# Another opening for the attention part of a two-stage kernel: where the first four outputs' upper score blocks come from, how the first z is fetched, and when w2 is loaded

## The chip, the cores and the metric

The kernel runs on one core of one Trainium2 chip. A core has a matrix engine (TensorE, PE in the profile; its weight loads are PEld), a vector engine (VectorE, DVE), a scalar engine (ScalarE, ACT), GpSimd (POOL) and a queue engine (SyncE, SP). Here POOL and SP do little but issue transfers. POOL's are made by software and can convert float32 to bfloat16 on the way; SP's are made by hardware and can transpose, but not convert. The metric is the device time of one execution in microseconds, as a median of several runs. The order of the instructions on each engine is the order of the program text: nothing is reordered by a planner, and each engine takes its instructions in that order and waits on semaphores.

## The reference

Eight batches b of 3136 rows. First an attention without softmax, in which z stands on both sides, then a mixer:

```python
scores = (1.0 / S) * np.matmul(z, z.transpose(0, 2, 1))   # (8, 3136, 3136), z has 64 columns
attn = np.maximum(scores, 0.0) ** 2
x = u * np.matmul(attn, v)                                # u, v: (8, 3136, 256)

h = x.transpose(0, 2, 1) @ U @ V                          # rank 32
y = x + h.transpose(0, 2, 1)
out = y + np.maximum(y @ w_ch1, 0.0) @ w_ch2              # 256 -> 1024 -> 256
```

The scores are symmetric: block (j, o) is the transpose of block (o, j). The kernel uses this.

## The kernel before

**Tiles and blocks.** The 3136 rows of a batch are 24 tiles of 128 rows and one tail of 64 (NT = 25, NF = 24, tile t = 24 is the tail). For each tile j a panel `A[j]` holds 13 blocks of 128 columns (NB = 13): the squared, rectified scores of tile j with tiles j, j+1, ..., j+12, counted modulo 25. The other twelve blocks that an output needs are transposes of blocks in its own panel. They come as a `strip` of 12 blocks: `turn(b, o)` (L311) has SP transpose `A[o]` by DMA into one of five strip buffers. `block(b, o, j)` (L345) picks the panel or the strip.

**Scores.** `score` (L272) makes a piece: two matmuls, one on each half of TensorE's rows, that run at the same time (that is why z is kept twice, in partitions 0 to 63 and 64 to 127), into one of two PSUM buffers (`ps2`, two banks each); then ACT rectifies and scales out of PSUM (L291) and VectorE squares in place (L293). A whole panel is two pieces of 832 columns (`score_steps`, L295). Products (`half`, L349, and `beside`, L601) take a block as weights and 256 columns of v as the moving side, again in two row halves. The two halves of TensorE add into two PSUM banks, and two outputs share a pair of banks; `sets` (L97) holds two such pairs. `close_pair` (L360) adds the two banks and multiplies by u: one ACT copy, two VectorE operations.

**z.** The matmuls need z transposed, in `zT` (25 tiles, and the first 12 again behind them, `extend_z` L217). `load_z` (L169) fetches z by POOL with conversion, `double_z` (L182) copies it twice on VectorE, and `turn_z` (L192) transposes by SP. For batch 0 `turn_on_pe` (L199) transposes by matmuls against the unit matrix `eye`, and ACT or VectorE copies the result out of PSUM. For batch 0 zT lies in `zT_first`, in room of `relu_bf` that is idle at that time; other batches use `zT_rest`.

**Order.** Outputs run in the order 12, 13, ..., 24, 0, ..., 11 (`turns`, L132). In each of the 25 steps i of a batch (L783) the products of one output are issued, with pieces of later panels spread between them. `turn(b, turns(i + 4))` is issued at the end of step i. From batch 1 on, the mixer of the batch before is done in bursts at steps 4, 8, 13 and 17; its second matmul, the first reader of w2, is at L562.

**The opening** (`start_up`, L607) is batch 0's first eight outputs, in two groups of four, before that loop begins at step 8 (output 20).
- Group 1, outputs 12 to 15: thirteen `pairs` (L642) of tiles j. For each, the scores of the two tiles j with the four outputs are made (512 columns each), and used two pairs later by four outputs at once. For j = 3 to 11 they are part of a panel and are put there. For the other sixteen (0, 1, 2 and 12 to 24) they are put into `rooms` (L639), in the v buffer of batch 1 and in `x_bf`, and are used only here; the panels of these tiles are made later all the same. Beside them five of the eight pieces of panels 16 to 19 are made (`nxt`).
- Group 2, outputs 16 to 19: the rest of `nxt`, six stored pairs, then a `tail` in which the strips' products, the pieces of panels 20 to 23 (`more`) and the rests of panels 8 to 15 (`rest`, 36 blocks) alternate. w2 is fetched when group 2 opens (L693), and z of batch 1 is doubled and turned whole just after (L695).
- `first_at` (L756) lists what is left for the loop: panels 24, 0, 1, 2, and the first blocks of panels 3 to 11.
- `v_at` (L781) spreads the nine loads of batch 1's v over steps 9 to 23.

Of the kernel before, what the change touches and what calls it, by code (L numbers as in the profile page):

```python
# [42 lines left out]
def kernel(  # L43
# [11 lines left out]
    nc = tc.nc  # L55
# [136 lines left out]
    def turn_z(b, parts):  # L192
        z_bf = z_tiles[b]
        for t0, t1 in parts:
            transpose(
                out=zT_of(b)[:, t0 : upto(t1), :],
                in_=z_bf[:, t0 : upto(t1), :, :].rearrange("p t h c -> p (t h c)"),
            )
    def turn_on_pe(parts, banks):  # L199

        z_bf = z_tiles[0]
        for (t0, t1), ps in zip(parts, banks):
# [8 lines left out]
            copy = nc.vector.tensor_copy if t0 % 8 else nc.scalar.copy  # L211
# [21 lines left out]
    def weight_steps():  # L233
# [21 lines left out]
        def copies():  # L255
# [7 lines left out]
            lambda: wide(w2_bf, moe_w_ch2),  # L263
# [343 lines left out]
    def start_up():  # L607
        parts = ((8, 16), (0, 8), (16, NF))
        load_z(0, parts[:2])
# [10 lines left out]
        load_v(0, (8, 12))  # L620
        load_v(0, (12, 18))
        load_z(0, parts[2:])
        for part in [(3, 8), (0, 3), (18, NF), (NF, NT)]:
            load_v(0, part)
        double_z(0, parts[:2])
        turn_on_pe([(8, 12), (12, 16)], sets[0])
        turn_on_pe([(0, 4), (4, 8)], sets[1])
        nc.gpsimd.memset(U_bf[:, NF, :], 0.0)
        outs = [FIRST + i for i in range(NG)]
        c0 = FIRST * P  # L630
# [5 lines left out]
        for s in fetches[:3]:  # L636
            s()
        nxt = [s for j in range(LEAD, LEAD + NG) for s in turned(0, j)]
        rooms = [v_both[1][:, t : t + 4, :] for t in range(0, NF, 4)]  # L639
        rooms = [r.rearrange("p (a t) d -> p a (t d)", a=2) for r in rooms]  # L640
        rooms += [x_bf[:, g].rearrange("p (a w) -> p a w", a=2) for g in (2, 3)]
        pairs = [(8, 9), (10, 11), (12, 13), (14, 15), (6, 7), (3, 4), (5,), (1, 2)]  # L642
        pairs += [(0, 16), (17, 18), (19, 20), (21, 22), (23, 24)]
        where = {}

        def make(pair):
            if all(LEAD - 1 - HALF <= j < FIRST for j in pair):
                todo = []
                for j in pair:
                    at = (FIRST - j) * P  # L650
                    where[j] = A[j][:, at : at + NG * P]
                    todo.append((j, c0, NG * P, where[j]))
                score(0, todo)
            else:
                room = rooms.pop(0)
                for i, j in enumerate(pair):
                    where[j] = room[:, i, :]
                score(0, [(j, c0, NG * P, room) for j in pair])

        seen = []  # L660

        def use(pair):
            for j in pair:
                for o in outs:
                    at = (o - FIRST) * P
                    stop = [o % 2 == 1 and len(seen) == NT - 1 - h for h in range(2)]
                    beside(o, j, where[j][:, at : at + P], stop)
                seen.append(j)

        for i, pair in enumerate(pairs):  # L670
            if i == 3:
                double_z(0, parts[2:])
            if i == 5:
                ps = pair_psum()
                turn_on_pe([(16, 20), (20, NF)], [ps[:, 0, :], ps[:, 1, :]])
                turn_on_pe([(NF, NT)], [pair_psum()[:, 0, :]])
                extend_z(0)
            make(pair)
            if i > 5 and i % 2:
                nxt.pop(0)()  # L680
            if i > 1:
                use(pairs[i - 2])
        for pair in pairs[-2:]:
            nxt.pop(0)()
            use(pair)
        for o in outs[1::2]:
            close_pair(0, o)
# [187 lines left out]
```

## Time and profile before

| | |
|---|---|
| median of 5 runs | 1015.0 us (1010.15 to 1024.21) |
| the profiled execution | 1013.82 us, its span 1012.1 us |
| PE busy | 991.3 us, 98% of the span |
| ACT busy | 613.8 us, 61% |
| DVE busy | 541.5 us, 54% |
| POOL busy | 172.1 us, 17% |
| chain that ended last | PE 91%, DVE 4%, DMA 2%, ACT 2% |
| products with panel blocks (L351) | 4864 matmuls, 334.6 us busy |
| products with strip blocks (L351) | 4420 matmuls, 306.6 us busy |
| scores (L278, `zT`) | 812 matmuls, 130.7 us busy |

The page gives busy time of each engine as a share of one profiled execution, the chain of waits that ended last, and groups of instructions by line and shape. A matmul's own duration in it (270 ns for a product) is not its price: matmuls overlap, and two row halves run at once, so a row of sixteen is what shows the rate. Durations beside an ACT or VectorE row in the timeline are those of a merged group: "x4" after 2.07 us means four instructions that ended 2.07 us after the first began. "[0.75 <-ACT A L291]" is the idle time of the engine before the row, and what ended it.

### The profile page before, as it was taken

How to read it: one execution, taken by the hardware profiler on the slowest of the kernel's cores; microseconds unless marked ns; L12 is line 12 of the kernel's file. 1: busy time of each engine (PE TensorE's matmuls, PEld its weight loads, DVE VectorE, ACT ScalarE, POOL GpSimd, SP SyncE). 2: the span in 40 equal slices, each digit the busy share in tenths (PEclk: the TensorE clock that was granted, in tenths of full speed). 3: DMA queues.
4: the chain of work that ended last, by engine and by line, in shares of the span. 5: the costliest groups of instructions: out<-in, count | busy, mean ns of one | idle time of the engine just before them, and what ended most of it. 6: DMA issues, size and time to landing. Idle time of an engine off the chain costs nothing.

```text
span 1012.1 us, 31331 instructions
## 1 busy us (share of the span) xinstructions
PE 991.3 (98%) x13856; PEld 783.5 (77%) x13856; DVE 541.5 (54%) x977; ACT 613.8 (61%) x834; POOL 172.1 (17%) x318
## 2 busy tenths in 40 slices
PE   7899999999999999999999999999999999999998
PEld 5678778787778877788787887878877788777856
DVE  5878654456544664446654556445664356542242
ACT  6887764667645776456764667556674666643154
POOL 4122112121121211121112211112112120011000
PEclk9999999999999999999999999999999999999999
DMA  8999989999898998989999998989999998767432
GB/s 156 158 204 222 180 147 194 177 176 155 156 202 170 176 168 171 163 183 171 148 187 165 183 167 146 190 172 189 151 159 194 172 181 142 140 148 166 103 97 97
DMA packets 414584, 167.70 MB, mean 166 GB/s; under 512 B 389408, under 2 KB 399328, under 8 KB 414448
## 3 DMA queue, kind: packets, MB, share of 16 engines
q1 hardware_dynamic: 384944, 99.16, 61.2%
q0 software_dynamic: 29504, 66.55, 28.2%
q8 instruction: 108, 1.77, 0.7%
q14 instruction: 28, 0.23, 0.1%
HBM read 61.88 MB, written 25.69 MB: 87 GB/s over the span
## 4 chain that ended last, share of the span: by engine, by line
PE 91%; DVE 4%; DMA 2%; ACT 2%; issue 1%; DVEq 0%; ACTq 0%; POOLq 0%
PE ps L351 46%; PE ps L562 17%; PE ps L520 17%; PE ps L278 6%; ACT A L291 1%; PE ps L385 1%; DVE A L293 1%; PE ps L442 1%; DVE x_bf L502 1%; DMA ut<-x_bf 1%; PE ps L488 1%; DVE both L366 1%; DMA zT<-z_bf 1%; DVE x_bf L375 0%; DMA strip<-A 0%
## 5 line engine op out<-in xcount | busy, mean ns | idle before, releaser
L291 ACT ACTIVATE A<-ps 128x832 bf16<-128x832 f32 (+8 forms) x469 | 352.8, 763 | 154.5 <-PE ps L278 146.0
L351 PE MATMUL ps<-v,A 64*128 64x256 bf16 x4864 | 334.6, 270 | 4.9 <-DVE A L293 2.8
L293 DVE TENSOR_TENSOR A<-A 128x832 bf16<-128x832 bf16 (+8 forms) x469 | 240.4, 524 | 147.8 <-ACT A L291 144.0
L351 PE MATMUL ps<-v,strip 64*128 64x256 bf16 x4420 | 306.6, 269 | 0.5 <-DMA strip<-A 0.5
L351 PEld LDWEIGHTS <-A 64*128 64x128 bf16 x4864 | 238.7, 94 | 49.5 <-issue 13.6
L538 ACT ACTIVATE relu_bf<-ps 128x1024 bf16<-128x1024 f32 (+2 forms) x208 | 187.9, 909 | 142.9 <-PE ps L520 140.9
L351 PEld LDWEIGHTS <-strip 64*128 64x128 bf16 x4420 | 220.6, 94 | 35.4 <-DMA strip<-A 0.9
L562 PE MATMUL ps<-w_bf,relu_bf 128*128 128x256 bf16 x1600 | 204.7, 273 | 0.2 <-ACT relu_bf L536 0.2
L573 DVE TENSOR_TENSOR o_sb<-ps,x_bf 128x512 f32<-128x512 f32 (+1 forms) x104 | 69.7, 670 | 246.8 <-PE ps L562 237.0
L520 PE MATMUL ps<-ut,w_bf 128*128 128x512 bf16 (+2 forms) x896 | 199.4, 353 | 0.9 <-DMA ut<-x_bf 0.5
L562 PEld LDWEIGHTS <-relu_bf 128*128 128x128 bf16 x1600 | 156.0, 98 | 47.2 <-issue 3.2
L335 POOL DMA_DIRECT2D u_sb<-in_u_dram x96 | 53.8, 560 | 470.0 <-DVE x_bf L375 437.0
L520 PEld LDWEIGHTS <-w_bf 128*128 128x128 bf16 x896 | 85.1, 98 | 61.8 <-issue 6.4
L278 PE MATMUL ps<-zT 64*128 64x416 bf16 (+8 forms) x812 | 130.7, 312 | 0.0
L365 ACT COPY both<-ps 128x512 f32<-128x512 f32 (+1 forms) x104 | 58.8, 566 | 73.2 <-PE ps L351 65.4
L581 POOL DMA_DIRECT2D out_dram<-o_sb x84 | 46.0, 547 | 270.2 <-DVE o_sb L573 266.2
L366 DVE TENSOR_TENSOR both<-ps,both 128x512 f32<-128x512 f32 (+1 forms) x104 | 69.3, 666 | 27.2 <-ACT both L365 26.6
L375 DVE TENSOR_TENSOR x_bf<-both,u_sb 128x512 bf16<-128x512 f32 (+1 forms) x104 | 69.8, 671 | 3.6
L502 DVE TENSOR_TENSOR x_bf<-ps,x_bf 128x512 bf16<-128x512 f32 (+1 forms) x112 | 65.4, 626 | 8.1 <-PE ps L488 8.1
L278 PEld LDWEIGHTS <-zT 64*128 64x128 bf16 x812 | 42.2, 94 | 4.0
L225 POOL DMA_DIRECT2D v<-in_v_dram x61 | 34.0, 559 | 0.2 <-PE ps L520 0.2
L278 PE MATMUL ps<-relu_bf 64*128 64x416 bf16 (+9 forms) x121 | 22.8, 351 | 2.4 <-ACT A L291 1.3
(52 smaller groups left out, 230.7 us busy)
## 6 DMA issues: line engine op xcount, KB each, us to landing
u_sb<-in_u_dram POOLq DMA_DIRECT2D x96, 256.0 KB, 3.8
out_dram<-o_sb POOLq DMA_DIRECT2D x84, 256.0 KB, 3.2
v<-in_v_dram POOLq DMA_DIRECT2D x57, 192.0 KB, 4.4
strip<-A SPq DMA_TRANSPOSE x196, 5.3
out_dram<-o_sb SPq DMA_DIRECT2D x12, 256.0 KB, 2.2
z_c<-in_z_dram POOLq DMA_DIRECT2D x7, 384.0 KB, 5.9
w_bf<-in_moe_w_ch_dram POOLq DMA_DIRECT2D x2, 512.0 KB, 7.5
u_sb<-in_u_dram POOLq DMA_DIRECT2D x16, 64.0 KB, 2.5
```

The costliest lines, as they stand in the source:

```text
L278: mm(out=ps[:, k, :n], lhsT=zT[halves[k], j, :], rhs=zT_flat[halves[k], c : c + n], start=True, stop=True,)
L291: nc.scalar.activation(out=dst, in_=src, func=AF.Relu, scale=sc)
L293: nc.vector.tensor_tensor(out=dst, in0=dst, in1=dst, op=ALU.mult)
L351: mm(out=acc[t0][h][:, (o - t0) * D : (o - t0 + 1) * D], lhsT=w[halves[h]], rhs=v_both[b % 2][halves[h], j, :], start=start, stop=stop, **kw,)
L365: nc.scalar.copy(out=both[:, :w], in_=banks[1][:, :w])
L366: nc.vector.tensor_tensor(out=both[:, :w], in0=banks[0][:, :w], in1=both[:, :w], op=ALU.add)
L375: nc.vector.tensor_tensor(out=x_at(b, t0, n), in0=split(both[:, :w]), in1=u_sb[:, :n, :].rearrange("p t (a c) -> p t a c", c=P), op=ALU.mult,)
L502: nc.vector.tensor_tensor(out=q, in0=split(ps[h][:, : len(ks) * D]), in1=q, op=ALU.add)
L520: mm(out=ps[i][:, :w] if apart else ps[:, i, :w], lhsT=w1_bf[:, db, (hp + i) * P : (hp + i + 1) * P], rhs=uT[c][:, db, len(chunks[c]) * P ...
L538: nc.scalar.activation(out=relus[c][:, hp : hp + 2, :w], in_=ps[:, :, :w], func=AF.Relu)
L562: mm(out=ps[:, k * D : (k + 1) * D], lhsT=relus[c][:, ht, q : q + P], rhs=w2_bf[:, ht, :], start=(ht == 0), stop=(ht == NH - 1),)
L573: nc.vector.tensor_tensor(out=o_sb[:p, :nk, :].rearrange("p t (a c) -> p t a c", c=P), in0=split(ps[:p, : nk * D]), in1=x_at(b, t, nk)[:p] ...
```

## The change

All of it concerns batch 0's opening and what is moved out of its way.

- `first_z` is new. VectorE clears 512 columns of `zT_rest`, and TensorE runs seven matmuls of 512 columns on them, whose result nothing reads. SP fetches z tiles 8 to 15 and 0 to 7 as float32 into the two buffers of u; VectorE converts them into the lower copy of z and ACT into the upper one.
- The third part of z (tiles 16 to 24) is loaded by POOL ahead of all of v. The order of v's parts changes.
- z of batch 1 is loaded as before, then U, V and w1; two parts of v of batch 1 follow at once. w2 is not loaded in the opening, but in two halves at steps 0 and 2 of batch 1.
- Group 1 has 24 steps in place of thirteen pairs. `stored` makes scores of two tiles j below 12 with the four outputs and puts them into the panels. `panel` makes one of the two pieces of a panel, 12 to 17, and turns it by SP from 16 on. `mirror` transposes blocks of `A[o]` on TensorE against `eye` into PSUM, from where VectorE copies them into output o's strip; there are 48 such blocks, in six steps. Nothing is put into `rooms`. The products of a step are issued two steps later. z tiles 16 to 24 are turned ahead of step 2, which makes the first piece of panel 12.
- At step 18 SP reads 8 elements of the second part of batch 1's v into a scratch tile, `mark`.
- Group 2 makes panels 18 to 22, four stored pairs, and the rests of panels 8 to 11 (10 blocks). z of batch 1 is doubled and turned in two parts, after its steps 10 and 12.
- `first_at` then leaves panels 23 and 24 whole and the first blocks of panels 0 to 11. Strips 23, 24 and 0 are turned in steps 8 and 9. Batch 1's other v parts are loaded at every second step from 9 to 21.

```diff
+    def first_z(parts):
+        z_bf = z_tiles[0] = stage.tile([P, NT, 2, dqk], BF16, name="z_bf")
+        wide = zT_rest[:, :4, :].rearrange("p t c -> p (t c)")
+        nc.vector.memset(wide, 0.0)
+        ps = pair_psum()
+        for _ in range(7):
+            mm(out=ps[:, 0, :], lhsT=zT_rest[:, 0, :], rhs=wide, start=True, stop=True)
+        landed = []
+        for t0, t1 in parts:
+            z_f = u_pool.tile([P, 2, D], FP32, name="u_sb").rearrange("p a c -> p (a c)")
+            z_f = z_f.rearrange("p (t c) -> p t c", c=dqk)
+            nc.sync.dma_start(out=z_f, in_=rows(z[0])[:, t0:t1, :])
+            landed.append(z_f)
+        for (t0, t1), z_f in zip(parts, landed):
+            nc.vector.tensor_copy(out=z_bf[:, t0:t1, 0, :], in_=z_f)
+            nc.scalar.copy(out=z_bf[:, t0:t1, 1, :], in_=z_f)
...
-            copy = nc.vector.tensor_copy if t0 % 8 else nc.scalar.copy
+            copy = nc.vector.tensor_copy if t0 % 8 or t1 == NF else nc.scalar.copy
...
-            lambda: wide(w2_bf, moe_w_ch2),
+            lambda: wide(w2_bf[:, NH // 2 :, :], moe_w_ch2[H // 2 :, :]),
+            lambda: wide(w2_bf[:, : NH // 2, :], moe_w_ch2[: H // 2, :]),
...
     def start_up():
-        parts = ((8, 16), (0, 8), (16, NF))
-        load_z(0, parts[:2])
+        first_z(((8, 16), (0, 8)))
         nc.gpsimd.memset(eye, 1.0)
...
-        load_v(0, (8, 12))
-        load_v(0, (12, 18))
-        load_z(0, parts[2:])
-        for part in [(3, 8), (0, 3), (18, NF), (NF, NT)]:
+        load_z(0, ((16, NF),))
+        for part in [(8, 12), (12, 18), (3, 8), (18, NF), (0, 3), (NF, NT)]:
             load_v(0, part)
-        double_z(0, parts[:2])
-        turn_on_pe([(8, 12), (12, 16)], sets[0])
-        turn_on_pe([(0, 4), (4, 8)], sets[1])
...
+        run(fetches[:3])
+        if B > 1:
+            for part in V_PARTS[:2]:
+                load_v(1, part)
+        turn_on_pe([(8, 12), (12, 16)], sets[0])
+        turn_on_pe([(0, 4), (4, 8)], sets[1])
+        extend_z(0)
+        double_z(0, ((16, NF),))
...
+        def mirror(*blocks):
+            def make():
+                flat = pair_psum().rearrange("p a w -> p (a w)")
+                c = 0
+                for o, m0, m1 in blocks:
+                    for m in range(m0, m1):
+                        mm(
+                            out=flat[:, c + (m - m0) * P : c + (m - m0 + 1) * P],
+                            lhsT=A[o][:, (m + 1) * P : (m + 2) * P],
+                            rhs=eye,
+                            start=True,
+                            stop=True,
+                        )
+                    c += (m1 - m0) * P
...
+                    nc.vector.tensor_copy(
+                        out=strips[0, o][:, m0:m1, :].rearrange("p m c -> p (m c)"),
+                        in_=flat[:, c : c + n],
+                    )
...
+        steps = [
+            stored((8, 9), first), stored((10, 11), first),
+            panel(12, 0), panel(12, 1), stored((6, 7), first),
+            panel(13, 0), panel(13, 1), stored((3, 4), first),
+            mirror((12, 0, 8)), panel(14, 0), mirror((13, 0, 8)), panel(14, 1),
+            stored((5, 2), first), stored((1, 0), first), panel(15, 0),
+            mirror((12, 8, 12), (13, 8, 12)), panel(15, 1), mirror((14, 0, 8)),
+            panel(16, 0), mirror((15, 0, 8)), panel(16, 1),
+            mirror((14, 8, 12), (15, 8, 12)), panel(17, 0), panel(17, 1),
+        ]
+        ends = ends_of([e for _, uses in steps for e in uses])
+        for n, (make, uses) in enumerate(steps):
+            if n == 2:
+                turn_on_pe([(16, 20), (20, NF), (NF, NT)], [*sets[0], sets[1][0]])
+            if n == 18 and B > 1:
+                nc.sync.dma_start(out=mark, in_=v_both[1][:1, V_PARTS[1][1] - 1, :8])
+            make()
+            if n > 1:
+                av(steps[n - 2][1], ends)
...
+        todo = [stored(js, LEAD) for js in ((11, 10), (9, 8), (7, 6), (5, 4))]
+        rest = [s for j in range(8, FIRST) for s in score_steps(0, j, LEAD + NG - j, NB)]
+        steps = [
+            (panel(18, 0)[0], []),
+            (panel(18, 1)[0], [(o, j) for j in sides for o in low]),
+            (panel(19, 0)[0], [(o, j) for j in sides for o in high]),
+            (panel(19, 1)[0], own[16] + own[17]),
+            (todo[0][0], []),
+            (todo[1][0], own[18] + own[19]),
...
+        ]
+        for k, s in enumerate(rest):
+            steps.append((s, mirrored[16][3 * k : 3 * k + 3]))
+        for k in range(4):
+            steps.append((panel(21 + k // 2, k % 2)[0], mirrored[17][3 * k : 3 * k + 3]))
+        for o in high:
+            steps.append((None, mirrored[o]))
...
+            if B > 1 and n in (10, 12):
+                part = ((0, FIRST), (FIRST, NF))[n // 2 - 5]
+                double_z(1, (part,))
+                turn_z(1, (part,))
...
-    first_at = {8: [(NT - 1, 0, NB), (0, 0, NB)], 9: [(1, 0, NB)], 10: [(2, 0, NB)]}
-    first_at.update({11: [], 12: []})
-    for j, i in zip(range(3, FIRST), (9, 10, 11, 11, 11, 12, 12, 12, 12)):
+    first_at = {8: [(NT - 2, 0, NB)], 9: [(NT - 1, 0, NB)], 10: [], 11: [], 12: []}
+    for j, i in enumerate((8, 10, 10, 11, 11, 11, 12, 12, 12, 12, 12, 12)):
         first_at[i].append((j, 0, FIRST - j))
+    first_turns = {8: (NT - 2,), 9: (NT - 1, 0)}
...
-        v_at = dict(zip((9, 11, 12, 14, 16, 18, 20, 22, 23), V_PARTS)) if b == 0 else {}
+        v_at = dict(zip((9, 11, 13, 15, 17, 19, 21), V_PARTS[2:]))
...
-            if i + AHEAD < NT:
+            if b == 0 and i in first_turns:
+                for t in first_turns[i]:
+                    turn(b, t)
+            elif i + AHEAD < NT:
                 turn(b, turns(i + AHEAD))
...
+            if b == 1 and i in (0, 2):
+                fetches.pop()()
```

## The prediction

> **What bounds the kernel now.** I read the engine shares first, then busy time in 4 us windows, the timeline of the first 60 us, and the chain that ended last. The page says that TensorE is the bound of the whole: PE 991.3 us of 1012.1, and 91% of the chain. The windows say that the opening is the exception:
>
> ```profile
> core 0: us, PE busy (x) PEld busy (x) DVE busy (x) ACT busy (x) POOL busy (x), PEclk, DMA share, GB/s
> 0.00:4.00 4.00, 0.00 (x0) 0.00 (x0) 0.00 (x0) 1.28 (x1) 2.82 (x10) 1.00 0.32 42
> ...
> 20.00:24.00 4.00, 3.48 (x50) 2.60 (x50) 3.16 (x5) 4.00 (x5) 0.00 (x0) 1.00 0.69 125
> 24.00:28.00 4.00, 3.94 (x66) 3.28 (x64) 3.04 (x5) 3.82 (x6) 0.00 (x0) 1.00 0.54 102
> 28.00:32.00 4.00, 2.02 (x30) 1.45 (x26) 3.51 (x7) 2.52 (x5) 0.58 (x1) 1.00 0.53 98
> 32.00:36.00 4.00, 2.04 (x25) 0.95 (x22) 3.95 (x8) 3.15 (x6) 1.45 (x2) 1.00 0.68 153
> ...
> 56.00:60.00 4.00, 4.00 (x74) 3.36 (x72) 2.84 (x7) 3.80 (x7) 0.00 (x0) 1.00 0.97 159
> ```
>
> From 56 us on PE is never idle. So the change is worth the shift of the moment from which that holds, plus the TensorE work that it adds later. Two marks are enough: the end of the first group of four outputs (196 value products of 49 per output) and of the second (392). Counted in the timeline, group 1 ends at 28.5 and the first product of output 20 starts at 50.74.
>
> ```profile
> 8.91 1.94 PE L351 MATMUL ps<-v,A 64*128 64x256 bf16 x16
> 11.04 1.94 PE L351 MATMUL ps<-v,A 64*128 64x256 bf16 x16
> 13.18 1.27 PE L351 MATMUL ps<-v,v 64*128 64x256 bf16 x16
> 16.46 1.05 PE L351 MATMUL ps<-v,v 64*128 64x256 bf16 x16
> ```
>
> The same sixteen products take 1.94 us until 13 us and 1.05 later: TensorE ran at half rate until then, although the windows' clock column says 1.00 throughout. The chain shows what else costs time:
>
> ```profile
> 1.30 3.03 DMA z_c<-in_z_dram
> ...
> 20.62 1.83 ACT v L291 x2
> 22.45 0.76 ACT A L291
> 23.21 0.93 ACT v L291
> ...
> 29.16 0.69 DVE both L366
> 30.49 0.69 DVE both L366
> 31.81 1.87 DVE z_bf L188 x2
> 33.68 1.85 DVE A L293 x4
> ```
>
> The first z ends 4.34 us in; ACT (doubled scores are the 1024-wide `v L291`) holds 18.8 to 24; closing group 1 and doubling the next batch's z on VectorE holds 28.5 to 35.5. Last, output 20 still waits:
>
> ```profile
> 52.87 0.72 PE L351 MATMUL ps<-v,A 64*128 64x256 bf16 x10 [1.19 <-DVE A L293]
> ```
>
> **Prices.** Back to back, ACT takes 0.744 us for 832 columns (6.70/9), 0.54 for 512 (1.08/2), 0.975 for 1024 (1.95/2). VectorE squares take 0.59, 0.42 and 0.69; its copy of 512 columns out of PSUM takes 0.69, and 1024 columns out of PSUM took 1.225 (the only such row, L479). A product is 0.0545 us (0.87/16). A transpose on TensorE: four in 0.40 us with the drain, so I take 0.062 and bound it by 0.053 and the cold 0.118 (1.89/16).
>
> **What each engine gains and loses to the end of group 2.**
> ACT before: group 1 has 8 doubled pairs 7.8, 9 stored blocks of 512 4.9, 5 panel halves 3.7, zT copies 0.9: 17.3. Group 2 has 11 halves 8.2, stored 5.7, parts of panels 8 to 15 (36 blocks) 4.3, closes 2.1: 20.3. After: group 1 5.7 + 12 halves 8.9 + 0.9 = 15.5; group 2 10 halves 7.4 + 3.5 + 10 blocks 1.3 + 2.1 = 14.3. Sum 37.6 to 29.8.
> VectorE before: 5.5 + 3.8 + 3.0 + z and copies 2.1 = 14.4, then closes 5.5 + z 1.9 + 6.5 + 4.6 + 3.6 = 22.1. After: 4.6 + 7.1 + mirrors (4 x 1.225 + 4 x 0.69 = 7.7) + 0.7 = 20.1, then 5.5 + 1.9 + 5.9 + 3.0 + 1.3 = 17.6. Sum 36.5 to 37.7. The mirrors give VectorE back all that the doubled squares took.
> TensorE: 8 x 0.213 = 1.7 us of doubled scores go, 48 transposes x 0.062 = 3.0 come. The seven new idle matmuls run while nothing else can.
>
> **The walk.** These loads don't run side by side freely, so I walk the steps. Rules, all from the code: every engine in its order; score n takes one of the two `ps2` buffers, free when the read of the step two before has ended; the products of step n-2 come after score n and wait for their square; a mirror holds its buffer until VectorE has copied it. Walking the old list this way from 4.92, with half rate to 13.6, gives 28.4 and 50.4 for the two marks, against 28.5 and 50.7 in the trace. The new list:
> - Start. z by SP: its 256 KB stores took 2.2 us against 3.8 for POOL's loads, so z near 3.0 and 3.8, casts 0.4 to 0.55 more. Seven 512-wide matmuls at half rate (0.427 each, twice the 0.213 of a pair) from 1.0 end at 4.0. Scores of step 0 end on PE at 6.4 (trace before: 7.9).
> - But step 2 is now panel 12, which needs z tiles 16 to 24, and VectorE doubles these (0.8) after the 0.63 copy that extends zT: done at 8.2. Their turn is queued on PE ahead of the first product, and its copies behind ACT's and VectorE's work of steps 0 and 1: ready 10.3. First product 10.5, against 8.91. Everything won before this point is lost in it; with z a microsecond earlier or 7 idle matmuls fewer the walk doesn't move.
> - Group 1: PE passes step 7 at 15.8, step 14 at 23.1, step 17 at 26.5, the end at 33.4. The loss is at mirrors: mirror 8 is copied until 18.3, mirror 10 until 20.3, and scores 10 and 12 wait for these buffers, so ACT is idle from 17.95 to 20.2. Hence 33.4 and not 28.4.
>   PE's time after steps 0 to 23: 6.4, 6.6, 11.4, 12.4, 13.1, 13.3, 15.3, 15.8, 16.3, 18.1, 19.8, 20.2, 21.5, 21.6, 23.1, 23.9, 24.2, 26.5, 26.7, 28.4, 28.6, 31.7, 31.9, 33.4; VectorE's after steps 8, 10, 12, 15, 17, 19, 21, 23: 18.3, 20.3, 22.2, 25.0, 28.5, 30.2, 32.3, 34.2. From the end of PE's work to its reader I count 0.19 (four transposes, 0.40), from ACT 0.12 (0.86 alone against 0.744), from VectorE 0.1.
> - Group 2: its first bank pair was free at 28, the second frees at 34.9 while products of the first run; the stalls at 28.5 to 35.5 go. Less ACT work, end at 49.4.
>
> **Sum.** 49.4 - 50.4 = -1.0. ACT and VectorE end 0.7 and 2.0 us behind PE there (before 1.7 and 3.2), so I take 1.0 of the 1.19 stall of output 20 away. Later, panels 23, 24 and 33 blocks of panels 0 to 2 remain where four panels did: +7 blocks, 0.2 on PE, 0.8 on ACT, which has room (3.80 of 4 falls with output 21's lighter list). Strips 20 to 22 queue on SP behind two halves of zT(1), where the whole took from 33.71 to about 45 beside the w2 load: 0 to 0.6, I take 0.2. The 8-element read into `mark` holds SP until two v parts land; strip 16 is next behind it on SP and is not due before 42 us, so nothing. w2 in halves at outputs 12 and 14 of batch 1, some 103 and 110 us, first read at 127; the two follow u loads on POOL and land in 7.5 each: nothing, and several us if they slipped past 127. v(1) parts move earlier but one, nothing reads them before 100 us. Casts on ACT (1.1) lie before its first score. Sum: -1.0 - 1.0 + 0.2 + 0.2 = -1.6.
> The profiled execution took 1013.8 (span 1012.1), 1.2 below the median of 1015.0. That gives 1012.2 on its basis, 1013.4 on the median's; I say 1012.5.
>
> Bounds, each walked: VectorE's copies at 0.9 or 1.45 per 1024: -1.1, +1.1. Half rate until 14: +2.1. Third z late by 3: +2.6. Handover shorter by 0.07: -0.8.
>
> **Two rules weighed.** The row on rate first: 1.94 against 1.05 until 13 us. The Trainium skill, page "TensorE: Matmul & The Clock Gate", Part 1, has the clock halved until a free-running window of about 3.4 us was busy, and halved again after an idle one. By it the idle matmuls would have it full by some 4.5 to 8 us, an estimate, though the walk leaves PE with gaps from 6.6 to 10.3. No row decides; after the thin stretch at 31 to 35 the next sixteen took 1.05, so gaps of 1 to 2 us didn't cost the rate here.
> Four transposes in 0.40 us is the other row. The same page, Part 4, gives about 275 ns for one transpose in a kernel. By it 48 would be 13.2 us, an estimate, 10 more than my sum, about 1022; that is for a transpose mode, and these are plain products with `eye`, so I go by the row.
>
> **Rivals.**
> 1. Faster: the mirrors don't hold the buffers (VectorE's copies overlap better than walked). VectorE then sets the end: 8.2 + 37.7 = 45.9 without any idle time, 4.8 below the mark of before; with the stall 6.0, so 1008. Against: VectorE is idle in every window before 28 us. A gain over 10 us would need less VectorE work than there is, so it takes scatter too. 22%.
> 2. Slower: VectorE stands still on the third z in front of the first squares. It decides once the third part and its two tails land after 7.5 us. In the trace this part was issued at 4.14 and read only at 11.24; it is now issued near 1.5, ahead of v, and the first part took 3.0. At 10 us it costs 2.6, and TensorE idle that long may be cold again, 2.1: end of group 2 at 54, +3.6 and the stall stays, 1017 to 1018. 18%.
> 3. Transposes dear (0.118 or more, not hidden): 48 x 0.056 = 2.7 at least, 1016, to 1022 and over. 5%.
> 4. The first z isn't earlier by SP. By the walk that changes nothing, so it has no case of its own.
>
> **The numbers.** Forecast 55%, by itself 1009 to 1016. Runs of before went from 1010.15 to 1024.21 about 1015, so a median of five can shift by 2 or 3. Range for 8 in 10: 1004.5 to 1019. What a measurement can tell from no change is about 1%, 10 us. Faster by more: half of rival 1 with scatter, 0.15. Slower by more: rival 3 and a little of 2, 0.08. Within: 0.77.
>
> **What would show it.** First product near 10.5 and group 1 later than before (about 33), group 2 at 49 to 50; the sixteens at 1.05 from the start; VectorE near 4 of 4 and ACT with holes between 16 and 30 us; no 1.19 stall at output 20. I'm wrong if the first product comes by 8 (then the turn of step 2 was mispriced), if group 1 ends before 30 (mirrors cheap), or if the windows after 56 us lose PE time (strips or w2 late).

## The result, and the profile after

| | before | after |
|---|---|---|
| median | 1015.26 us (75 runs, 1009.41 to 1027.78) | 1025.15 us (38 runs, 1018.26 to 1037.35) |
| ratio | 1 | 1.009 [1.0073, 1.0107] |
| the profiled execution | 1013.82, span 1012.1 | 1026.04, span 1024.3 |
| PE busy | 991.3 | 998.8 |
| chain that ended last | PE 91%, DVE 4%, DMA 2%, ACT 2% | PE 88%, DVE 4%, DMA 4%, ACT 3% |

The change makes the kernel 0.9% slower, about 10 us. 1012.5 was predicted, and the measured time lies above the range.

Where do 12 us of the profiled execution come from? Counting value products in the timeline (49 for each output) gives the start of each output; the mark of output 21 is its product with the tail, which is issued at the end of output 20's step. First products, in us:

| output | before | after | difference |
|---|---|---|---|
| 12, the first | 8.91 | 9.39 | +0.5 |
| 16, group 2 | 29.89 | 34.96 | +5.1 |
| 20, the loop | 50.74 | 50.18 | -0.6 |
| 21 | 55.49 | 56.35 | +0.9 |
| 24 | 65.31 | 66.24 | +0.9 |
| 0 | 68.04 | 70.47 | +2.4 |
| 3 | 77.00 | 79.44 | +2.4 |
| 8 | 92.78 | 104.65 | +11.9 |
| batch 1 | 104.73 | 116.59 | +11.9 |
| batch 7 | 840.59 | 852.65 | +12.1 |

The opening itself is 0.6 us ahead when it ends. Everything is lost afterwards, in the 17 outputs of batch 0's loop, where PE was almost never idle before (48.31 of 49.5 us). Busy time in two stretches, the opening's second half and the loop, in the kernel before:

```profile
core 0: us, PE busy (x) PEld busy (x) DVE busy (x) ACT busy (x) POOL busy (x), PEclk, DMA share, GB/s
20.00:50.50 30.50, 25.02 (x362) 19.00 (x363) 24.69 (x48) 27.02 (x43) 2.59 (x4) 1.00 0.94 148
50.50:100.00 49.50, 48.31 (x851) 39.71 (x852) 39.21 (x74) 39.01 (x58) 11.46 (x19) 1.00 1.20 214
```

and after, with some single windows of 4 us in the second fence:

```profile
20.00:50.50 30.50, 26.33 (x406) 21.29 (x402) 25.45 (x50) 21.55 (x37) 1.09 (x2) 1.00 0.74 127
50.50:100.00 49.50, 40.38 (x658) 33.24 (x655) 31.72 (x61) 29.90 (x46) 10.50 (x17) 0.95 1.18 177
```

```profile
24.00:28.00 4.00, 3.09 (x45) 2.16 (x44) 3.59 (x5) 1.34 (x3) 0.00 (x0) 1.00 0.11 18
28.00:32.00 4.00, 2.33 (x38) 1.77 (x38) 3.56 (x6) 1.80 (x3) 0.54 (x1) 1.00 0.17 45
32.00:36.00 4.00, 3.69 (x54) 2.60 (x51) 3.04 (x6) 2.88 (x5) 0.00 (x0) 1.00 0.58 119
...
56.00:60.00 4.00, 3.65 (x64) 3.29 (x66) 0.61 (x2) 1.78 (x3) 0.00 (x0) 1.00 1.12 152
...
84.00:88.00 4.00, 2.44 (x23) 1.91 (x24) 2.03 (x4) 2.69 (x4) 0.00 (x0) 0.65 1.16 148
```

The last two columns carry the reading. In the loop PE loses 8 us of busy time while the transfer engines are as full as before (1.18 against 1.20), but they move 177 GB/s in place of 214. In the opening they were left idle: 0.11 and 0.17 at 24 to 32 us, where before had 0.54 and 0.53, because the first strip that SP can turn (output 16) is ready at 31.78 and not at 23.86. The chain of waits of the same execution names the transfers:

```profile
47.52 3.07 PE ps L371 x57
50.59 5.71 DMA strip<-A
...
56.35 1.04 PE ps L371 x15
...
71.44 0.84 PE ps L371 x15
72.28 12.44 DMA strip<-A
...
84.80 0.71 ACT A L311
85.56 0.53 PE ps L298 x2
86.09 1.12 PE ps L371 x11
87.21 11.09 DMA strip<-A
...
98.39 1.03 ACT A L311
```

A row "DMA strip<-A" is a strip's turn from its issue to its landing: 12.4 and 11.1 us here. Who stands still for it, in the timeline and in the sums of waits from 72 to 106 us:

```profile
84.80 2.21 ACT L311 ACTIVATE A<-ps 128x640 bf16<-128x640 f32 x3 [4.42 <-DMA strip<-A]
85.56 0.53 PE L298 MATMUL ps<-zT 64*128 64x416 bf16 x2 [3.24 <-ACT A L311]
...
91.09 0.81 ACT L311 ACTIVATE A<-ps 128x768 bf16<-128x768 f32 x1 [3.59 <-DMA strip<-A]
...
98.39 2.54 ACT L311 ACTIVATE A<-ps 128x1024 bf16<-128x1024 f32 x3 [3.02 <-DMA strip<-A]
```

```profile
ACT A L311 <- DMA strip<-A: 12.2, 4, 4.4
```

From output 0 on, pieces of batch 1's panels are made between batch 0's products, and they overwrite `A[o]` of batch 0. ACT may not write until the strip of the panel has been read out. So a late strip stops ACT, ACT holds the two `ps2` buffers, and PE stands behind it. At 50.59 the wait is more direct: products want strip 21, which SP issued only then, after the two halves of zT(1) at 46.07 and 48.92.

### The profile page after: what moved, and what is told of

Read it like the earlier page. It is cut to its first block, busy times and chain, and to the rows that moved or that the text cites. A ratio compares the mean times of both kernels' runs of the same rounds, so it can differ in the third digit from the quotient of the medians.

```text
span 1024.3 us, 31437 instructions
## 1 busy us (share of the span) xinstructions
PE 998.8 (98%) x13902; PEld 791.5 (77%) x13902; DVE 543.3 (53%) x981; ACT 608.7 (59%) x831; POOL 171.6 (17%) x317
## 4 chain that ended last, share of the span: by engine, by line
PE 88%; DVE 4%; DMA 4%; ACT 3%; issue 0%; POOL 0%; ACTq 0%; DVEq 0%
PE ps L371 44%; PE ps L582 17%; PE ps L540 17%; PE ps L298 6%; DMA strip<-A 3%; ACT A L311 2%; DVE A L313 1%; PE ps L462 1%; PE ps L405 1%; DVE x_bf L522 1%; PE ps L508 1%; DVE both L386 1%; DVE x_bf L395 1%; DMA ut<-x_bf 1%; DMA u_sb<-in_u_dram 0%
## 5 line engine op out<-in xcount | busy, mean ns | idle before, releaser
L311 ACT ACTIVATE A<-ps 128x832 bf16<-128x832 f32 (+9 forms) x472 | 353.1, 761 | 172.5 <-PE ps L298 153.2
L371 PE MATMUL ps<-v,A 64*128 64x256 bf16 x4896 | 338.9, 271 | 0.5 <-DVE relu_bf L231 0.5
L313 DVE TENSOR_TENSOR A<-A 128x832 bf16<-128x832 bf16 (+9 forms) x472 | 241.3, 523 | 159.9 <-ACT A L311 156.3
L371 PE MATMUL ps<-v,strip 64*128 64x256 bf16 x4512 | 313.4, 269 | 2.5 <-DMA strip<-A 2.5
L371 PEld LDWEIGHTS <-A 64*128 64x128 bf16 x4896 | 244.3, 95 | 42.8 <-issue 11.5
L371 PEld LDWEIGHTS <-strip 64*128 64x128 bf16 x4512 | 227.3, 94 | 36.7 <-DMA strip<-A 3.0
L298 PE MATMUL ps<-relu_bf 64*128 64x416 bf16 (+10 forms) x112 | 21.4, 329 | 3.0 <-ACT A L311 2.3
```

What stands on the lines that cost most here:

```text
L298: mm(out=ps[:, k, :n], lhsT=zT[halves[k], j, :], rhs=zT_flat[halves[k], c : c + n], start=True, stop=True,)
L311: nc.scalar.activation(out=dst, in_=src, func=AF.Relu, scale=sc)
L313: nc.vector.tensor_tensor(out=dst, in0=dst, in1=dst, op=ALU.mult)
L371: mm(out=acc[t0][h][:, (o - t0) * D : (o - t0 + 1) * D], lhsT=w[halves[h]], rhs=v_both[b % 2][halves[h], j, :], start=start, stop=stop, **kw,)
```

## The experiments

Three theories stood at the start. A: the overwriting is the root; without it late strips would do no harm. B: the strips are slow because loads for batch 1 fall on the same steps. C: the profiled execution was an accident. Two more came with e_vearly. D: transposes on SP and loads on POOL, when both have work waiting, each run at a fraction of their own rate. E: SP's queue is late when the loop begins and never catches up. The table has what was measured, ratios to executions of the kernel before that were taken beside each run (their medians are 1014.62 to 1015.65); "b1" is the first product of batch 1 in the profiled execution, whose own time is beside it.

| run | median us | ratio | b1 | profiled |
|---|---|---|---|---|
| before | 1015.26 | | 104.73 | 1013.82 |
| b_same | one run | | 105.63 | 1015.2 |
| after | 1025.15 | 1.009 [1.0073, 1.0107] | 116.59 | 1026.04 |
| r_same | one run | | 116.68 | 1027.47 |
| e_later | 1025.96 | 1.0115 [1.0047, 1.0183] | 121.18 | 1034.62 |
| e_vlate | 1025.48 | 1.0121 [1.005, 1.0191] | 110.80 | 1022.17 |
| e_fill | 1019.41 | 1.0046 [1.0008, 1.0083] | 110.00 | 1019.89 |
| e_vearly | 1019.14 | 1.0048 [1.0026, 1.0069] | 111.31 | 1024.69 |
| e_zlate | 1019.87 | 1.0044 [1.0015, 1.0073] | 109.02 | 1017.64 |
| b_extra | 1021.63 | 1.007 [1.0029, 1.0111] | 109.96 | 1020.37 |
| b_firstz | 1020.52 | 1.004 [1.0018, 1.0063] | 113.58 | 1023.42 |
| e_noidle | one run | | 120.22 | 1033.33 |
| c_all | 1013.92 | 0.9995 [0.997, 1.0019] | 103.52 | 1013.22 |
| c_best | 1016.07 | 1.0008 [0.9987, 1.0028] | 108.23 | 1018.89 |
| c_extra | 1019.3 | 1.0028 [1.0001, 1.0055] | 107.84 | 1027.26 |

In all but the last row the profiled time less b1 is 908.6 to 913.4: what happens before batch 1 decides nearly the whole difference. c_extra's (919.4) lost time elsewhere. Executions of one kernel scatter by 10 to 20 us, so where b1 and a median disagree (e_vlate), the median counts.

**The changed kernel again** (no edit).

> The changed kernel unaltered, for a second trace. Theory A (ACT's scores of batch 1 go into panels that the strip transposes of batch 0 still read, and these take 11 to 13 us from issue to landing there, against 6 to 8 before): ACT again stands 3 to 4.5 us at a time on strip transposes between 79 and 102 us, some 8 us lost, batch 1 begins near 116.6 and not near 104.7. Theory C (that trace was an odd one): the stalls lie elsewhere or are gone, batch 1 begins below 110.

Long steps stood at outputs 20, 24, 3 and 4 again (8.6 us for output 3, 7.1 in the first trace), but at 21 in place of 6 and 7. b1 came within 0.1 us, which is in part chance, since the waits were spread otherwise. C falls. A second trace of before (b_same) had b1 at 105.63.

> The kernel before unaltered, for a second trace. If its opening and loop keep away from the collapse by their spacing and not by luck: batch 1 begins at 104 to 106 us again, strips in batch 0's loop land in 6 to 8 us. If the first trace was a lucky one: batch 1 begins at 107 or later, with ACT or TensorE waits on strips.

**Batch 1's pieces one output later** in batch 0's loop, so that panels are overwritten later.

```diff
+    next_first = {i: [] for i in range(NT)}
+    for i in range(NT):
+        next_first[min(i + 1, NT - 1)] += next_at[i]
...
-                fill += [s for key in next_at[i] for s in score_steps(b + 1, *key)]
+                at = next_at if b else next_first
+                fill += [s for key in at[i] for s in score_steps(b + 1, *key)]
```

> The changed kernel, but in batch 0 the scores of batch 1 are made one output (about 3.2 us) later than listed. Theory A: the strips have 3.2 us more before they are in the way, so most of the ACT stalls of 79 to 102 us go: 5 to 9 us faster than the changed kernel, 1016 to 1021. Theory B (the strips are slow because loads of v and u of batch 1 fall on the same steps, and whatever waits for a strip is late): the strips are as slow, and the time moves by less than 3 us, since the products of the strips wait too.

The waits from 45 to 125 us:

```profile
PE ps L371 <- DMA strip<-A: 13.9, 4, 6.7
ACT A L311 <- DMA strip<-A: 10.2, 3, 7.2
```

Theory A falls: the products themselves now wait for strips, up to 6.7 us at once. The strips are late for whoever reads them; the overwriting is only the first to notice.

**v at the steps of before.** No part of batch 1's v in the opening, no `mark`.

```diff
-            for part in V_PARTS[:2]:
-                load_v(1, part)
...
-        v_at = dict(zip((9, 11, 13, 15, 17, 19, 21), V_PARTS[2:]))
+        v_at = dict(zip((9, 11, 12, 14, 16, 18, 20, 22, 23), V_PARTS))
```

> The changed kernel with all nine parts of batch 1's v loaded in the loop at the steps of the kernel before (9, 11, 12, 14, ...), and without the two early ones and the small read that SP waits on. Theory B: strips land in 6 to 8 us again between 70 and 100 us and 6 to 9 us come back, 1016 to 1019. Theory A, and the loads don't matter: within 3 us of the changed kernel, 1023 to 1028.

The profiled execution was 4 us quicker and its batch 1 began 5.8 earlier; the median of the four executions was not lower (1025.48). The 6 to 9 us that B promised didn't come. With an interval of 1.005 to 1.0191 a smaller gain isn't excluded.

**Pieces of panels 3, 6 and 7 one or two steps earlier**, for the 1.5 us that output 24's step had grown by (4.23 us against 2.73).

```diff
-    for j, i in enumerate((8, 10, 10, 11, 11, 11, 12, 12, 12, 12, 12, 12)):
+    for j, i in enumerate((8, 10, 10, 9, 11, 11, 11, 11, 12, 12, 12, 12)):
```

> The changed kernel with the first blocks of panels 3, 6 and 7 made at steps 9, 11 and 11, as in the kernel before, and not at 11 and 12. The step of output 24 took 4.23 us against 2.73 in the kernel before, with six pieces beside it against four: if ACT's work there is the cause, 1.5 us come back (1024, and 2.8 us for that step). Theory A says nothing of it beyond that, theory B the same; 0 if the stall there is a strip.

Output 24's step is 2.73 us again. The median falls by 6, more than the 1.5 that were expected of the step, but its interval (1.0008 to 1.0083) overlaps with after's (1.0073 to 1.0107), so the rest of the 6 isn't shown.

**All of batch 1's v in the opening**, none in the loop.

```diff
-            for part in V_PARTS[:2]:
+            for part in V_PARTS:
                 load_v(1, part)
...
-                nc.sync.dma_start(out=mark, in_=v_both[1][:1, V_PARTS[1][1] - 1, :8])
+                nc.sync.dma_start(out=mark, in_=v_both[1][:1, NF - 1, :8])
...
-        v_at = dict(zip((9, 11, 13, 15, 17, 19, 21), V_PARTS[2:]))
+        v_at = {}
```

> The changed kernel with all of batch 1's v loaded in the opening, ahead of the first strip (SP's small read then waits on the last full part), and none in the loop. Theory D (strip transposes and POOL's loads, when both have work waiting, each run at a fraction of their own rate: 0.29 MB a microsecond for strips alone, about 0.1 for both together between 78 and 101 us): with half of the loads gone from there, strips land in 4 to 8 us, ACT's 3 to 5 us stalls on strips go, batch 1 begins near 107 to 109, time 1015 to 1019. Theory E (SP's queue is simply a strip and a half late when the loop begins and never catches up): 1022 to 1027.

The time is 6.0 us below after's, close to D's range and below E's. From 80 to 105 us strips land in 4 to 7 us, and the waits from 45 to 125 us shrink where the loads are gone; strip 21 is no earlier than it was:

```profile
PE ps L371 <- DMA strip<-A: 3.5, 1, 3.5
ACT A L311 <- DMA strip<-A: 2.4, 1, 2.4
```

**The kernel before with more transfers, and with an earlier start.** First, three needless 8-block turns (two strips' worth) on SP at the end of group 2:

```diff
+        for o in (19, 20, 21):
+            ut = ut_pool.tile([P, ND * 512], BF16, name="ut")
+            transpose(out=ut.rearrange("p (t c) -> p t c", c=P), in_=A[o][:, P : 9 * P])
```

> The kernel before, with three transposes of 8 blocks each (two strips' worth, into a free tile, read by nothing) put on SP at the end of group 2, which makes its queue about as late at the loop's start as in the changed kernel. Theory E: products and scores of batch 0 then wait on strips as in the changed kernel, 4 to 10 us slower than before (1019 to 1025). If the queue's lateness is not what matters: within 2 us of before, since SP's queue is free for some of the time there.

Second, before with `first_z` alone:

```diff
     def start_up():
-        load_z(0, parts[:2])
+        first_z(parts[:2])
...
-        double_z(0, parts[:2])
```

> The kernel before with the new fetch of z and the seven idle matmuls alone. In the changed kernel's trace TensorE's clock is full from 6.7 us, but half again from 10.1 to 13.5, where its queue stood still for z tiles 16 to 24; the old list has no such gap. So group 1 should run at full rate from about 7 us: first product at 8.0 and not 8.9, o = 16 begins at 27 to 28.5 and not 29.9; 1 to 2.5 us faster than before in all, if the strips are not disturbed. Rival: ACT bounds group 1 from 18 us on in any case, and nothing is left at o = 16.

Both are slower, by 0.7 and 0.4%. In b_extra products wait for strips, as E has it, and once that is paid at outputs 24 and 0, every step takes as long as in before again, to 0.01 us:

```profile
PE ps L385 <- DMA strip<-A: 3.2, 1, 3.2
```

The second is the telling one: output 12 starts 1.2 us earlier, output 16 3.3 and output 20 2.2, and yet batch 1 begins 8.9 later, with 13.6 us of ACT waiting in five waits from 45 to 125 us:

```profile
ACT A L309 <- DMA strip<-A: 13.6, 5, 4.0
```

Getting PE sooner to the loop is worth nothing by itself. At a fixed pace of the transfers only the 2.2 us would have gone; that batch 1 comes 8.9 later goes with transfers that move half as much in the same time. From 70 to 80 us in b_firstz, and then in before (the columns are those of the first table of windows, the last two the DMA share and GB/s):

```profile
70.00:80.00 10.00, 7.88 (x136) 6.72 (x131) 5.91 (x10) 4.33 (x7) 1.43 (x3) 1.00 1.30 123
```

```profile
70.00:80.00 10.00, 10.00 (x180) 8.55 (x178) 7.96 (x17) 7.11 (x11) 2.56 (x4) 1.00 1.22 248
```

**One small idle matmul in place of seven.**

```diff
-        for _ in range(7):
-            mm(out=ps[:, 0, :], lhsT=zT_rest[:, 0, :], rhs=wide, start=True, stop=True)
+        mm(out=ps[:, 0, :P], lhsT=zT_rest[:, 0, :], rhs=zT_rest[:, 0, :], start=True, stop=True)
```

> The changed kernel with one small idle matmul in place of seven. If the idle matmuls bring the clock early, it is now granted in full only some 3.4 us later or more (after 10 us and not from 6.7), the second half-rate stretch (10.1 to 13.5) merges with the first, and the mark of o = 16 (34.5 to 35.0) moves by less than 1 us, because the first product waits for z tiles 16 to 24 until 10.25 either way. If they matter: o = 16 later by 1.5 us or more.

Matmuls run at full rate from 11.8 us in place of 6.7, and output 16 comes 0.9 us sooner (34.06 against 34.96). So the seven matmuls gain nothing there, as walked. The one execution's loop was worse (b1 at 120.22); with one run nothing is concluded from that.

**Transfers alone.** This program leaves out the whole computation: eight strips by SP, then eight v loads of three tiles by POOL, then eight of each together.

```diff
+    for j in range(N):
+        strip(j)
+        load(1, j)
```

> Leaves out the whole computation and times transfers alone: first eight strip transposes (12 blocks each) on SP, then eight loads of 3 v tiles on POOL, then eight of each issued together. From the traces strips alone run at 0.29 MB a microsecond, so 1.35 us each, about 11 us and a start; loads alone took about 1.0 us each, 8 us and a start. Theory D (the two hinder each other): together clearly longer than the sum of the two alone, 30 us or more. Rival (they share the sixteen engines fairly, and the slowness in the kernel comes from something else): together no longer than the sum, 22 us or less.

Alone, eight strips took 16.8 us and eight loads 11.8, more than the 11 and 8 expected. Together they took 28.2, against a sum of 28.6; that lies between the two marks set for it. But they don't share it by need. The queues (packets, MB, share of 16 engines) while strips ran alone, from 1.7 to 18.5 us:

```profile
q1 hardware_dynamic: 12544, 3.15, 100.1%
```

and beside loads, from 34 to 44 us:

```profile
q0 software_dynamic: 1039, 1.43, 93.1%
q1 hardware_dynamic: 1002, 0.25, 21.9%
```

q1 is SP's queue, q0 POOL's. In these 10 us one packet of the one goes for one of the other. Nearly all of a strip's packets have 256 bytes and most of a load's 1536, so strips fall from 747 to 100 packets per us, and one of 1568 packets needs some 16 us; the second strip of this part took 16.7 from issue to landing, where 4.2 was the median alone. The Trainium skill, page "DMA: Bandwidth & Descriptors", section "Queues, rings and completion order", has each transfer engine take turns between its queues packet by packet, where a packet is a group of some 9 to 17 descriptors. 1039 against 1002 agrees with it if the profile's packets are these, which no run here shows. From 44 to 49 us, while the last loads landed, it was otherwise:

```profile
q1 hardware_dynamic: 1428, 0.36, 122.0%
q0 software_dynamic: 113, 0.14, 15.8%
```

Share x 16 engines x length / packets gives the time of a packet: 68 ns for a strip's here, 35 from 34 to 44 us and 21 alone. The two queues moved 100 GB/s, against 168 before it and 187 for strips alone. The loads were through at 48.86 and the strips at 59.28:

```profile
48.86 0.29 DVE L111 CAST o_sb<-v 128x256 f32<-128x256 bf16 x1 [17.01 <-DMA v<-in_v_dram]
59.28 0.23 DVE L112 CAST o_sb<-strip 128x128 f32<-128x128 bf16 x1 [10.13 <-DMA strip<-A]
```

So D isn't settled: over this whole part no throughput is lost, in 5 us of it nearly half is, and the strips behind the loads, 8704 packets in 10.3 us, made up for it. What stands is that for ten of these us strips gave way to pending loads. How full the engines are can be estimated from these prices. Per pair of outputs the loop needs two strips (2.1 each), a v part (1.5 x 0.86 = 1.3 us of all engines) and a u load (1.7, an estimate: v's by bytes, 256 KB against 192), together 7.2 us of engine time. PE takes 6.35 per pair in before ((104.73 - 50.74) / 17 x 2). If a share of 1.20, as in before's loop, counts for what it says, 7.2 fit into 6.0, with almost no slack; but 1.15 to 1.18 in the mixed part above gained almost nothing, so this is no more than an estimate. It can't mean that what is late stays late: in b_extra above and e_zlate below the loop keeps before's pace once a wait has paid for the lateness.

**Batch 1's z turned after strip 22**, not ahead of strip 21.

```diff
-                turn_z(1, (part,))
...
+            if B > 1 and n == 17:
+                turn_z(1, ((0, FIRST), (FIRST, NF)))
```

> The changed kernel with batch 1's z transposed by SP after strip 22 and not between strips 20 and 21. Strip 21 then lands some 5 us sooner: the 2.5 us wait of TensorE in output 21 goes, and with it the half-rate stretch that followed it in three of the four altered kernels; the steps of outputs 20 and 21 take 3.7 and 3.3 us (6.2 and 3.0 in the changed kernel). Theory E alone would bring batch 1 back by more than 5 us; theory D leaves the waits after 79 us as they are, so 2 to 4 us in all, 1021 to 1023.

Outputs 20 and 21 take 3.3 and 3.1 us. The wait reappears as 4.7 us for strip 23, the first behind z:

```profile
PE ps L371 <- DMA strip<-A: 4.7, 1, 4.7
```

From output 0 on every step takes as long as in before, to 0.01 us, so the waits after 79 us are gone, which D had staying; batch 1 begins 7.6 us sooner, more than the 5 that E asked for. The strip of an output's partner is read one output earlier than its number says: the two products with the tail are issued together at the end of the first of the two outputs (L443 and L445 of after).

**The three together**: e_vearly, e_fill and e_zlate in one kernel.

> The changed kernel with all three: batch 1's v early, the first blocks of panels as in the kernel before, z of batch 1 turned after strip 22. Each term as seen singly: 5.3 by v, 1.5 by the blocks, 2 to 4 by z. Batch 1 begins at 105 to 108 us and the time is 1012 to 1017, about that of the kernel before; if the terms are the same wait seen three times, 1017 to 1020.

0.9995 [0.997, 1.0019]: the loss is gone. Windows of the two stretches:

```profile
20.00:50.50 30.50, 26.33 (x408) 21.67 (x405) 25.72 (x52) 22.54 (x39) 6.41 (x13) 1.00 1.05 180
50.50:100.00 49.50, 46.97 (x831) 40.05 (x828) 37.52 (x73) 36.45 (x55) 5.54 (x9) 1.00 1.13 195
```

The opening's transfers are now at 1.05 (0.74 in after), which is work that the loop doesn't have to do, and the loop's clock is 1.00. One direct wait is left:

```profile
60.56 0.28 PE L371 MATMUL ps<-v,strip 64*128 64x256 bf16 x1 [2.53 <-DMA strip<-A]
```

**Taking that wait away**: c_all with z turned after strip 23, in the loop's step 8.

```diff
-            if B > 1 and n == 17:
-                turn_z(1, ((0, FIRST), (FIRST, NF)))
...
+                if i == (11 if b else 13):
...
+                if i == 8 and more:
+                    turn_z(1, ((0, FIRST), (FIRST, NF)))
```

> The combination of before (v early, blocks as before) with batch 1's z turned on SP only after strip 23, at step 8, and its first twelve tiles copied behind it at step 13, not 11. In the combination TensorE still stood 2.5 us for strip 23, which is due at the end of output 22 and came behind z. If that was only the order on SP: that wait goes, batch 1 begins at 101 to 102 us (103.5 in the combination), 1011 to 1013, 2 to 4 us faster than the kernel before. If the transfers as a whole are the bound in the loop, the wait reappears at a later strip and nothing is gained: 103 to 104.

Strip 23's wait is gone, outputs 20 to 23 take 3.2 to 3.6 us each, and other waits for strips have taken its place, from 45 to 125 us:

```profile
ACT A L311 <- DMA strip<-A: 4.7, 3, 2.3
...
PE ps L405 <- DMA strip<-A: 1.7, 1, 1.7
```

The same kernel with the three needless turns of b_extra:

> The same, with three redundant transposes of 8 blocks (two strips' worth, 4 to 5 us of transfers) on SP at the end of group 2, as in the altered kernel before that lost 5.2 us at batch 1's begin. If the loop's transfers are the bound there (strips, u and v together near all of the time), taking v out leaves room and the added strips cost clearly less than there: 0 to 2.5 us. If lateness of the queue alone decides, as much as there, 4 to 6 us.

Here they moved b1 by nothing (107.84 against 108.23), although the loop began 1.9 us sooner, and the median by 3.2 us, with intervals that overlap. That lies between the two ranges. It doesn't settle whether c_best's loop is still bound by transfers.

No version beat the kernel before. c_all equals it: its opening runs 2.9 us ahead at output 20 (47.84), and all but 1.2 us of this is gone by batch 1 (103.52).

## Why the prediction was wrong

**The premise failed.** "From 56 us on PE is never idle. So the change is worth the shift of the moment from which that holds." PE was never idle there because strips arrived just in time, and that depended on the transfers made in the opening. b_firstz moves this moment by -2.2 and the kernel gets 0.4% slower; b_extra leaves PE's work as it is and makes it 0.7% slower. The profile had the sign of it: windows with a DMA share of 0.97 at 56 to 60 us, and 1.20 over the loop, for which the sum had no term.

**The term that was mis-sized**: "Strips 20 to 22 queue on SP behind two halves of zT(1) ... 0 to 0.6, I take 0.2". At output 21 the position against before is +0.9, where the sum had -1.8 (-1.0 - 1.0 + 0.2). 0.4 of these 2.7 us arose in the opening (-0.6 for -1.0), the rest in output 20's step. It takes 6.2 us in after and 3.3 in e_zlate, which undoes this order: the term was 2.9, not 0.2. The prediction doesn't say when strip 21 is due. It is needed at the end of output 20 (L445), and SP issued it at 50.59 (47.76 in before); strip 20 still stands ahead of z. In the outputs after it, where no wait was priced at all, late strips cost the rest: 9.5 us between outputs 3 and 8, besides 1.5 at output 24, of another kind (below). e_zlate also shows why moving the order alone is no cure: the wait goes to strip 23.

**"v(1) parts move earlier but one, nothing reads them before 100 us."** True of who reads v, and beside the point: e_vearly, which takes the loads out of the loop, wins 6 us (1019.14 against 1025.15). This cost had no place in the sum, which counted readers and not who shares the engines. In the stall itself the packets are also slower. SP's and POOL's queues in after, from 72.3 to 84.8 us:

```profile
q1 hardware_dynamic: 4305, 1.08, 76.0%
q0 software_dynamic: 423, 0.82, 40.8%
```

and in before from 72 to 84:

```profile
q1 hardware_dynamic: 6063, 1.52, 79.7%
q0 software_dynamic: 528, 1.18, 39.9%
```

Share x 16 engines x length / packets gives 35 and 193 ns for a packet in after, 25 and 145 in before. So both queues moved less at about the same share, as from 44 to 49 us with transfers alone, and this goes with the longest stalls: from 80 to 90 us 133 GB/s in r_same and 91 in e_later, 212 in before, at shares of 1.17 to 1.28. In the four kernels that load no v in the loop (e_vearly and the three whose names begin with c_) none of the four windows of 10 us from 60 to 100 with a share above 1 is below 155. But in before, with all nine loads there, none is below 186, so the loads of v alone don't bring it about.

**"+7 blocks, 0.2 on PE, 0.8 on ACT, which has room."** It hadn't at output 24's step: +1.5 us, and e_fill, which spreads the pieces, brings the step back to 2.73.

**"gaps of 1 to 2 us didn't cost the rate here."** In after's opening the rate fell behind such gaps, 1.34 us at 8.31 and the 0.53 below:

```profile
10.25 1.86 PE L371 MATMUL ps<-v,A 64*128 64x256 bf16 x15 [0.53 <-DVE relu_bf L231]
12.07 1.85 PE L371 MATMUL ps<-v,A 64*128 64x256 bf16 x16
...
15.48 1.05 PE L371 MATMUL ps<-v,A 64*128 64x256 bf16 x16
17.13 0.62 PE L686 MATMUL ps<-eye,A 128*128 128x128 bf16 x8
25.95 0.62 PE L686 MATMUL ps<-eye,A 128*128 128x128 bf16 x8 [0.75 <-DVE strip L699]
31.31 0.61 PE L686 MATMUL ps<-eye,A 128*128 128x128 bf16 x8 [1.67 <-DVE strip L699]
```

The seven idle matmuls had the clock up at 6.7, and it fell to half from 10.1 to 13.5, so that sixteen products took 1.85 once more. The gaps alone don't decide it. In e_zlate, with the same instructions up to there and gaps of 1.38 and 0.53, the clock came up at 5.0 and stayed:

```profile
9.93 1.03 PE L371 MATMUL ps<-v,A 64*128 64x256 bf16 x15 [0.53 <-DVE relu_bf L231]
```

Half rate also follows long waits of the loop, at 85.2 to 88.6 and 98.9 to 102.3, part of what each wait cost; a wait of 2.49 us at 56.35 cost no rate in after, one of 2.42 at the same place in r_same did. The Trainium skill, page "TensorE: Matmul & The Clock Gate", Part 1, gives a window of 3413 ns; each of these stretches is 3.4 long.

**Right**: the opening as walked. The first steady product comes at 10.25 (10.5 walked), and the row above names VectorE's copy of z tiles 20 to 23, turned for step 2, as walked. Group 1's last product starts 5.9 later (34.25 against 28.40; 5.0 walked), because mirrors hold the buffers that VectorE empties: "0.75 <-DVE strip" and "1.67 <-DVE strip" above, and ACT at 1.34 and 1.80 of 4 us. That 5.9 is near 5.0 is in part luck: the half rate is in it, which the sum left out ("the sixteens at 1.05 from the start"), and without it, in e_zlate, the product starts at 32.35, 3.9 later than in before. Output 20 starts 0.6 earlier (1.0 walked); four traces with this opening have it at 47.99 to 50.18, two of before at 50.74 and 51.65. Eight transposes take 0.62 with the drain, so rival 3 and the page's 275 ns each are out; ACT's holes speak against rival 1, and nothing waited for the third z, so rival 2 didn't happen. What would show it wrong, "if the windows after 56 us lose PE time (strips or w2 late)", is what came; for strips it needed a case of its own, with a price, and got none.

**How sure.** Shown: the loss arises in batch 0's loop; strips are late there for every reader; three edits that ease transfers or spread work win about 6, 6 and 5 us each against after (e_fill's 6 not clear of its interval) and 11 together, which undoes it. Their shares don't add, so no single one is the cause. For strip 21 the reason is shown, the order on SP. Open: why in the longest stalls both queues move about half as much at the same share, whether the loads of v bring this about, and whether c_best's loop is still bound by transfers.

## What to carry to other kernels

A PE without idle time says nothing about what comes next to it: look at the transfer share of the stage that a change hands over to, work out its transfers' engine time against its PE time, and where the two are close, count the transfers that the opening did for it as part of the opening's work. An edit that frees an engine early but leaves transfer engines idle there (0.94 to 0.74 here) can move the cost into the next stage. For each strip or tile ask when its first reader comes in the code, not which output it is named for.

## What the runs showed of the hardware

- Transposes on SP give way to pending loads on POOL: from 34 to 44 us of m_dma they got 1002 packets against 1039 of six times the size, 100 per us in place of 747, and one strip took 16.7 us from issue to landing, 4.2 alone. The whole part lost no time (28.2 us against 16.8 + 11.8).
- Transfer engines can be full and move half as much: 123 GB/s at a share of 1.30 in b_firstz, 248 at 1.22 in before, in the same 10 us; 100 in 5 us of m_dma. What brings it about is open.
- TensorE fell to half rate for 3.4 us after waits of 3.2, 2.7 and 2.4 us, and once in the opening behind gaps of 1.34 and 0.53 us; a wait of 2.49, and the same two gaps in e_zlate, left the rate full.
- Two strips' worth of needless turns, an estimated 4.2 us of the engines' time (2.1 a strip in m_dma), cost 6 us of the median in before (b_extra) and 3 in c_extra, there within the intervals.
